# Unit 0 moves into the loop: decode attention and a Mish MLP, regrouped into even–odd passes

## The chip, the cores and the metric

The kernel runs on one core of a Trainium2 chip. Its time is device microseconds of one execution; the span is the part of it from the core's first to its last instruction. The engines named below are TensorE (PE), VectorE (DVE), ScalarE (ACT), GpSimd (POOL) and SyncE (SP). SP computes nothing here: it runs through its own list of instructions in order, and nearly every transfer from device memory is one of its instructions.

## The reference

One decode step for 8 sequences, everything in float32. `x` is 8 x 512; there are 32 query heads, 8 key/value heads, 8192 cached positions, and a head dimension of 128.

```python
xn = layernorm(x)
q  = xn @ wq                                    # 8 x 32 heads x 128
p  = softmax(q . k_cache * 128**-0.5)           # 4 query heads share one key head
a  = (p . v_cache) @ wo
h  = xn @ w1 + b1                               # 512 -> 1792
m  = (h * tanh(softplus(h))) @ w2               # Mish, 1792 -> 512
out = x + a + m
```

Each of the two caches is 268 MB and is read once; all weights together are some 24 MB.

## The kernel before, in words

**Units.** The caches are cut into 32 units, each of one sequence and two key/value heads. A unit has one key tile and one value tile of 128 x 16384 floats, 8.39 MB each, and each is one transfer. For a unit `u` the kernel does: `scores` (32 matmuls of 512 columns over the key tile, in two halves of 16, `part` 0 and 1), `softmax` (maximum, exponential, sums), `turn` (four matmuls and vector transposes that bring the weights into `pt8`), then `values` (32 matmuls over the value tile), then `merge` (division by the sum, into `oT`). `key_weights` lays the queries of the next unit out into the one buffer `wk`.

**Places.** One buffer `kv` of 160 KB per partition holds everything that is loaded. In units of one tile (`ROW`): the value place `V_AT` is 0 to 1; the keys of even units are at `K_AT[0]`, 1 to 2, those of odd units at `K_AT[1]`, 1.5 to 2.5. The two key places share half a tile, so a key tile may be loaded as soon as the first half of the scores of the unit before it has read the shared part; that is why `scores` is in two parts with the load between them.

**Order.** The schedule is written by hand. In a pass `t` of the loop SP meets, in order: the load of keys, the load of values, again keys, again values, with a wait ahead of each for the matmuls that still read the place. After unit 0, which stands ahead of the loop with `mish` (hidden layer of the MLP, 32 matmuls over `w1` and about 15 vector operations), a pass is an odd unit `2t+1` (`unit(t, 0, ..)`) and an even unit `2t+2` (`unit(t, 1, ..)`); in the last of the 16 passes the even unit is replaced by `last()`: values of unit 31, `wo` and `w2`. `values` of a unit run one unit later, behind the scores of the next: value tile `2t` is read in `unit(t, 0)`, and its successor `2t+1` is loaded right behind that.

**How waits are counted.** Each transfer of the loop adds 16 to one of eight counts when it has landed. The counts (`DMAHW0` to `DMAHW7` in the listings below, with `_I-..._own` for those of the loop and `_49` for those of the code ahead of it) are dealt out to the transfers of the program in turn, at build time. Every pass has to raise every count by the same amount. Where a block under an `If` has transfers and isn't taken, the other side of the branch makes up for them on SP: for each count it first waits until the transfers that the program has before on the same count have landed, then adds what the left-out block would have added.

**Ahead of the loop.** SP issues `x`, half of `wq`, key tile 0 (into the value place, L153), `w1` (into the first key place, L518), then key tile 1 into `K_AT[1]` and value tile 0 into `V_AT` (both at L534, in `load`).

Of the kernel before, what the change touches and what calls it, by code (L numbers as in the profile page):

```python
# [13 lines left out]
P = 128  # L14
# [41 lines left out]

V_AT = 0
K_AT = (ROW, ROW + ROW // 2)
W1_AT = ROW
W2_AT = 2 * ROW  # L60
PLACES = 2 * ROW + ROW // 2

# [14 lines left out]
def kernel(  # L77
# [72 lines left out]
    for lo in range(0, FG, FG // 2):  # L150
        hi = lo + FG // 2
        nc.scalar.dma_start(b1_sb[:, lo:hi], b1.rearrange("(g f) -> g f", g=G)[:, lo:hi])
    nc.sync.dma_start(kv[:, V_AT : V_AT + ROW], kT[:NB].rearrange("j p f -> (j p f)").rearrange("(p f) -> p f", p=P))  # L153
    w1_t = kv[:, W1_AT : W1_AT + 7168].rearrange("p (i f) -> p i f", i=W1R)


# [153 lines left out]
            nc.scalar.copy(qr[:, at].rearrange("p i c -> p (i c)"), X[:, half])  # L310

    wk = const.tile([P, DI, 2, NH * G, REP], F32, name="wk")
    lsel = const.tile([P, 2, H2], F32, name="lsel")
    qT = const.tile([P, H2 * B], F32, name="qT")

    def key_weights(b, parts=1):
        w = wk
        q = qr.rearrange("p i (d o h b) -> p i d o h b", d=2, o=1, b=B)[..., b]
        n = DI // parts
        for i in range(0, DI, n):  # L320
            nc.vector.tensor_mul(  # L321
                w[:, i : i + n],
                q[:, i : i + n].to_broadcast([P, n, 2, NH * G, REP]),
                mask.rearrange("p (o d k r) -> p o d k r", o=1, d=2, r=1).to_broadcast(
                    [P, n, 2, NH * G, REP]
                ),
            )


    def scores(j, k, first, part):  # L330

        w = wk
        lo = 0 if first else DI // 2
        kk = k.rearrange("p (i c f) -> p i c f", i=DI, c=HALF)
        for n in range(DI // 2):
            i = lo + n
            for c in range(HALF):
                nc.tensor.matmul(  # L338
                    S[64 * c : 64 * (c + 1), :],
                    w[:, i].rearrange("p d k h -> p (d k h)"),  # L340
                    kk[:, i, c, :],
                    start=(part == 0 and n == 0),
                    stop=(part == 1 and n == DI // 2 - 1),
                )

    E, RT = {}, {}

    def softmax(j):
        nm = work.tile([P, 1], F32, name="nm")
# [11 lines left out]
    def turn(j):  # L361
        e = E.pop(j)
        for g in range(4):
            nc.tensor.matmul(X[:, g], perm[:, g], e, start=True, stop=True)  # L364
        if j % 2 == 1:

            n = 2 * H2
            nc.tensor.matmul(  # L368
                M[:, 136 : 136 + n], ones, lsel.rearrange("p u h -> p (u h)"), start=True, stop=True
            )  # L370
            rt = work.tile([P, 2, H2], F32, name="rt")
            nc.vector.reciprocal(rt.rearrange("p u h -> p (u h)"), M[:, 136 : 136 + n])  # L372
            RT[0], RT[1] = rt[:, 0], rt[:, 1]
        for tl in range(TL):
            nc.vector.transpose(  # L375
                tr.rearrange("p (l t) c -> p t l c", t=TL)[:, tl],
                X.rearrange("p g (t q l) -> p t l g q", t=TL, q=PP)[:, tl],
            )
        t = tr.rearrange("p y (k z) -> p y k z", k=2)
        nc.vector.tensor_add(t[:, :, 0], t[:, :, 0], t[:, :, 1])  # L380
        for d in range(2):
            half = slice(64 * d, 64 * (d + 1))
            t = tr[half].rearrange("p y (g c h) -> p g y c h", g=4, c=HALF)
            nc.vector.tensor_add(  # L384
                pt8[half, :, :, d * REP : (d + 1) * REP].rearrange("p c y h -> p y c h"),
                t[:, 0],
                t[:, 1],
            )


    def values(vt):
        for n in range(NJ):
            l, c = divmod(n, HALF)
            q = n % G
            nc.tensor.matmul(  # L395
                O[Q * q : Q * (q + 1), :],
                pt8[:, c, TL * l : TL * (l + 1), :].rearrange("p t h -> p (t h)"),
                vt[:, 512 * n : 512 * (n + 1)],
                start=(n < G),
                stop=(n >= NJ - G),  # L400
            )
        os = work.tile([P, DH], F32, name="os")
        nc.vector.tensor_scalar(os, O[:, :DH], isel[:, 0:1], None, op0=ALU.mult)  # L403
        for i in range(1, TL):
            nc.vector.scalar_tensor_tensor(  # L405
                os, O[:, DH * i : DH * (i + 1)], isel[:, i : i + 1], os, op0=ALU.mult, op1=ALU.add
            )
        return os

    def merge(os, u, b):  # L410
        nc.tensor.matmul(M[:, 168 : 168 + H2], os, hsel, start=True, stop=True)  # L411
        nc.vector.tensor_mul(oT[:, :, b], M[:, 168 : 168 + H2], RT[u])

    def turn_o(m):

# [108 lines left out]
    def place(at):  # L524
        return kv[:, at : at + ROW]
# [7 lines left out]
    def load(name, at, m, b):  # L533
        nc.sync.dma_start(place(at), units[name][m, b])  # L534

    load("k", K_AT[1], 0, 1)
    scores(0, place(V_AT), True, 0)
    scores(0, place(V_AT), False, 1)
    softmax(0)
    load("v", V_AT, 0, 0)  # L540
    key_weights(1)
    mish(w1_t, b1_sb, kv[:, W1_AT : W1_AT + 6 * FG])
    turn(0)

    def last():

        w_o = [kv[:, 4096 * m : 4096 * (m + 1)] for m in range(NP)]
        for m in range(NP):
            rows = wo[4 * m : 4 * (m + 1)].rearrange("u p f -> (u p f)")
            rows = rows.rearrange("(p f) -> p f", p=P)  # L550
            nc.sync.dma_start(w_o[m], rows)
        w2_rows = w2.rearrange("j p f -> (j p) f").rearrange("(q i) f -> q (i f)", i=W2R)
        w2_t = []
        parts = ((0, G, 0, G), (G, 8, 0, G), (8, 11, 0, G), (11, 13, 0, G), (13, 14, 0, 2), (13, 14, 2, G))
        for lo, hi, g0, g1 in parts:
            a, z = (lo * D, hi * D) if g1 - g0 == G else (lo * D + g0 * P, lo * D + g1 * P)
            t = kv[:, W2_AT + a : W2_AT + z]
            nc.sync.dma_start(t, w2_rows[:, a:z])  # L558
            w2_t.append(t)

        os = values(place(K_AT[0]))
        for m in range(NP):
            if m == 1:
                merge(os, 1, B - 1)
                turn_o(NP - 1)
            outputs(m, w_o[m])
        down_long(w2_t[0])
        a_sb = work.tile([P, 512], F32, name="e", bufs=1)
        nc.scalar.copy(a_sb, H)
        for g in range(G):  # L570
            nc.tensor.matmul(
                O[Q * g : Q * g + B, :P],
                bsel[:, :B],
                a_sb[:, g * P : (g + 1) * P],
                start=True,
                stop=False,
            )
        for p, t in zip(parts[1:], w2_t[1:]):
            down(p[0], p[1], t, p[2], p[3])
        res = work.tile([P, DH], F32, name="os")  # L580
        nc.vector.tensor_add(res, O[:, :P], xres)  # L581
        nc.sync.dma_start(out, res)

    def unit(t, p, more):

        j = 1 + p
        scores(j, place(K_AT[(1 + p) % 2]), p == 0, 0)
        if p == 0:
            with tc.If(t < LOOPS - 1) as here:
                load("k", K_AT[0], (2 * t + 2) // B % NP, (2 * t + 2) % B)  # L590
            with here.Else():
                load("v", K_AT[0], NP - 1, B - 1)
        else:
            load("k", K_AT[1], (2 * t + 3) // B % NP, (2 * t + 3) % B)
        scores(j, place(K_AT[(1 + p) % 2]), p == 1, 1)
        softmax(j)
        os = values(place(V_AT))
        if p == 0:
            with tc.If(t % 4 == 0):
                turn_o((t // 4 + NP - 1) % NP)  # L600
            with tc.If(t < LOOPS - 1):
                load("v", V_AT, (2 * t + 1) // B % NP, (2 * t + 1) % B)
            with tc.If(more == 3):  # L603
                spread()
        else:
            load("v", V_AT, (2 * t + 2) // B % NP, (2 * t + 2) % B)
        key_weights((2 * t + 2 + p) % B)
        if p == 0:
            with tc.If(more == 2):  # L609
                project(tr.rearrange("p y c -> p (y c)")[:, :512])  # L610
        else:
            with tc.If(more == 1):
                load_q((t // 4 + 1) % NP)
        turn(j)
        merge(os, p, (2 * t + p) % B)

    with tc.For_i(0, LOOPS, hint_engines=(), iteration_sync="reg_based") as t:
        more = t % 4 + (t // 12) * 4
        unit(t, 0, more)
        with tc.If(t < LOOPS - 1) as here:  # L620
            unit(t, 1, more)
        with here.Else():
            last()


# [36 lines left out]
```

## Time and profile before

| | |
|---|---|
| median of three runs | 1315.33 us (1311.61 to 1317.71) |
| profiled execution, own time | 1311.87 us |
| its span | 1310.1 us |
| PE busy in the span | 1002.2 us, 77% |
| DVE busy | 359.2 us, 27% |
| bytes moved | 561.36 MB, mean 428 GB/s |

The profile is of one execution, with 1.8 us of its own time outside the span. An engine's busy time is a share of the whole span. The DMA figures are means over the core's 16 DMA engines, among which every transfer is split.

### The profile page before, as it was taken

The page shows a single profiled execution, that of the slowest core. Times are in us where ns is not written, and L with a number is a line of the kernel's source. Part 1 is how long each engine was busy: PE and PEld are TensorE (multiplying, and loading weights), DVE is VectorE, ACT ScalarE, POOL GpSimd, SP SyncE. Part 2 cuts the span into 40 slices and gives each one's busy share as a digit, 9 for nine tenths or more (in the row PEclk, how much of TensorE's full clock was granted, in tenths as well). Part 3 has the DMA queues.
Part 4 walks back from the last instruction along what each step waited for, and adds up shares of the span by engine and source line. Part 5 has one row for each costly group of instructions (what it writes and reads, how often), then busy time and mean ns, then how long its engine had stood idle before and what let it go on. Part 6 is the DMA issues. An engine that isn't in the chain of part 4 may idle for free. (4 is left out here: it accounts for less than half of the span.)

```text
span 1310.1 us, 13984 instructions
## 1 busy us (share of the span) xinstructions
PE 1002.2 (77%) x4948; PEld 348.9 (27%) x4948; DVE 359.2 (27%) x654; ACT 39.3 (3%) x89; POOL 2.3 (0%) x10
## 2 busy tenths in 40 slices
PE   5688687777877688687697877679688777868676
PEld 2233222222322222232232322223222222223222
DVE  3422232221323312233131323312233240323312
ACT  1000000000000000000000000000000000000000
POOL 0000000000000000000000000000000000000000
PEclk9898797988888898778797989788888897988788
DMA  9989999999999999999999999999999999999998
GB/s 405 443 377 425 437 430 433 432 431 434 431 431 434 426 440 424 442 424 446 422 440 426 436 430 436 434 430 436 430 436 428 434 430 440 430 434 434 430 423 349
DMA packets 11715, 561.36 MB, mean 428 GB/s; under 512 B 1312, under 2 KB 1704, under 8 KB 1968
## 3 DMA queue, kind: packets, MB, share of 16 engines
q1 hardware_dynamic: 11536, 560.03, 99.0%
q10 hardware_dynamic: 160, 1.06, 0.2%
q8 instruction: 15, 0.25, 0.1%
q14 instruction: 4, 0.03, 0.0%
HBM read 561.01 MB, written 0.07 MB: 428 GB/s over the span
## 5 line engine op out<-in xcount | busy, mean ns | idle before, releaser
L338 PE MATMUL s<-kv,wk 128*64 128x512 f32 x2048 | 530.7, 660 | 183.3 <-DMA kv<-in_kT 106.8
L338 PEld LDWEIGHTS s<-kv,wk 128*64 128x64 f32 x2048 | 176.8, 151 | 501.1 <-issue 415.7
L395 PE MATMUL o<-kv,pt 128*32 128x512 f32 x2048 | 254.1, 653 | 30.9 <-DMA kv<-in_v 26.1
L350 DVE TENSOR_REDUCE nm<-s 128x1 f32<-128x512 f32 x32 | 22.1, 692 | 548.0 <-issue 369.9
L364 PE MATMUL x<-e,perm 128*128 128x512 f32 x256 | 131.0, 659 | 17.9 <-PEq L609 15.9
L395 PEld LDWEIGHTS o<-kv,pt 128*32 128x32 f32 x2048 | 66.7, 119 | 194.6 <-issue 159.9
L375 DVE STREAM_TRANSPOSE tr<-x 128x512 f32<-128x512 f32 x128 | 80.3, 685 | 2.1
L364 PEld LDWEIGHTS x<-e,perm 128*128 128x128 f32 x256 | 51.0, 210 | 95.6 <-issue 88.8
L321 DVE TENSOR_TENSOR wk<-qr,mask 128x1024 f32<-128x1024 f32 (+1 forms) x34 | 64.8, 1905 | 33.2 <-DVEq L603 15.3
L403 DVE TENSOR_SCALAR os<-o,isel 128x128 f32<-128x128 f32 x32 | 11.2, 351 | 227.5 <-PE o L395 200.7
L358 ACT ACTIVATE e<-s,nmx 128x512 f32<-128x512 f32 x32 | 22.0, 687 | 1129.4 <-DVE nmx L355 1129.4
L384 DVE TENSOR_TENSOR pt<-tr 64x512 f32<-64x512 f32 x64 | 43.9, 686 | 2.2
L380 DVE TENSOR_TENSOR tr<-tr 128x1024 f32<-128x1024 f32 x32 | 39.2, 1225 | 1.1
L351 PE MATMUL m<-ident,nm 128*128 128x128 f32 x64 | 17.8, 364 | 26.3 <-DVE nm L350 26.3
L405 DVE SCALAR_TENSOR_TENSOR os<-o,isel,os 128x128 f32<-128x128 f32 x96 | 33.7, 351 | 3.4
L351 PEld LDWEIGHTS m<-ident,nm 128*128 128x128 f32 x64 | 10.9, 214 | 65.9 <-DVE nm L350 65.9
L303 PE MATMUL x<-tr,gwide 128*128 128x512 f32 x16 | 15.7, 1079 | 13.4 <-DVE tr L298 10.5
L275 PE MATMUL h<-ws,xn 128*8 128x512 f32 x64 | 10.9, 761 | 6.5 <-PEq L603 5.2
L359 DVE TENSOR_SCALAR lsel<-rsel,l 128x8 f32<-128x8 f32 x32 | 7.4, 231 | 29.8 <-ACT e L358 29.8
L411 PE MATMUL m<-hsel,os 128*128 128x8 f32 x64 | 10.9, 243 | 5.7 <-DVE rt L372 5.6
L353 DVE TENSOR_TENSOR far<-m,apart 128x128 f32<-128x128 f32 x32 | 9.3, 292 | 20.7 <-PE m L351 20.7
L411 PEld LDWEIGHTS m<-hsel,os 128*128 128x128 f32 x64 | 10.8, 189 | 15.3 <-issue 7.2
(103 smaller groups left out, 148.3 us busy)
## 6 DMA issues: line engine op xcount, KB each, us to landing
kv<-in_wo SPq DMA_DIRECT2D x4, 2048.0 KB, 20.2
ws<-in_wq SPq DMA_DIRECT2D x3, 2048.0 KB, 32.4
kv<-in_w SPq DMA_DIRECT2D x1, 3584.0 KB, 35.3
kv<-in_w SPq DMA_DIRECT2D x2, 1024.0 KB, 28.1
ws<-in_wq ACTq DMA_DIRECT2D x1, 1024.0 KB, 5.1
ws<-in_wq SPq DMA_DIRECT2D x1, 1024.0 KB, 7.2
kv<-in_w SPq DMA_DIRECT2D x1, 768.0 KB, 26.4
kv<-in_kT SPq DMA_DIRECT2D x32, 28.8
```

What stands on the lines that cost most here:

```text
L321: nc.vector.tensor_mul(w[:, i : i + n], q[:, i : i + n].to_broadcast([P, n, 2, NH * G, REP]), mask.rearrange("p (o d k r) -> p o d k r", o ...
L338: nc.tensor.matmul(S[64 * c : 64 * (c + 1), :], w[:, i].rearrange("p d k h -> p (d k h)"), kk[:, i, c, :], start=(part == 0 and n == 0), s ...
L350: nc.vector.tensor_reduce(nm, S, axis=AX.X, op=ALU.max, negate=True)
L351: nc.tensor.matmul(M[:, 0:P], nm.to_broadcast([P, P]), ident, start=True, stop=True)
L358: nc.scalar.activation(e, S, AF.Exp, bias=nmx, accum_out=l)
L364: nc.tensor.matmul(X[:, g], perm[:, g], e, start=True, stop=True)
L375: nc.vector.transpose(tr.rearrange("p (l t) c -> p t l c", t=TL)[:, tl], X.rearrange("p g (t q l) -> p t l g q", t=TL, q=PP)[:, tl],)
L380: nc.vector.tensor_add(t[:, :, 0], t[:, :, 0], t[:, :, 1])
L384: nc.vector.tensor_add(pt8[half, :, :, d * REP : (d + 1) * REP].rearrange("p c y h -> p y c h"), t[:, 0], t[:, 1],)
L395: nc.tensor.matmul(O[Q * q : Q * (q + 1), :], pt8[:, c, TL * l : TL * (l + 1), :].rearrange("p t h -> p (t h)"), vt[:, 512 * n : 512 * (n ...
L405: nc.vector.scalar_tensor_tensor(os, O[:, DH * i : DH * (i + 1)], isel[:, i : i + 1], os, op0=ALU.mult, op1=ALU.add)
L411: nc.tensor.matmul(M[:, 168 : 168 + H2], os, hsel, start=True, stop=True)
```

## The change

Unit 0 is no longer ahead of the loop. A pass is now the even unit `2t` (`unit(t, 0)`) and the odd unit `2t+1` (`unit(t, 1)`), so 16 passes hold all 32 units, and `last()` stands at the end under an `If` of its own that only pass 15 takes. What pass 0 must not do (values and merge of the unit before) or alone has to do (`mish`) is under an `If` too. The first key tile goes to the even keys' place, `w1` to the value place, and `mish` takes its work space in `ws`, where the query weights were. `os` and `rt` are fixed buffers now, since their readers stand in another pass.

```diff
-W1_AT = ROW
+W1_AT = 0
...
-    nc.sync.dma_start(kv[:, V_AT : V_AT + ROW], kT[:NB]...)
+    nc.sync.dma_start(kv[:, K_AT[0] : K_AT[0] + ROW], kT[:NB]...)
...
-    load("k", K_AT[1], 0, 1)
-    scores(0, place(V_AT), True, 0)
-    scores(0, place(V_AT), False, 1)
-    softmax(0)
-    load("v", V_AT, 0, 0)
-    key_weights(1)
-    mish(w1_t, b1_sb, kv[:, W1_AT : W1_AT + 6 * FG])
-    turn(0)
...
     def unit(t, p, more):
+        k = place(K_AT[p])
+        scores(k, p == 1, 0)
         if p == 0:
+            load("k", K_AT[1], (2 * t + 1) // B, (2 * t + 1) % B)
+        else:
             with tc.If(t < LOOPS - 1) as here:
                 load("k", K_AT[0], (2 * t + 2) // B % NP, (2 * t + 2) % B)
             with here.Else():
                 load("v", K_AT[0], NP - 1, B - 1)
-        else:
-            load("k", K_AT[1], (2 * t + 3) // B % NP, (2 * t + 3) % B)
+        scores(k, p == 0, 1)
+        softmax(p)
+        if p == 0:
+            with tc.If(t > 0):
+                values(place(V_AT))
+        else:
+            values(place(V_AT))
...
             with tc.If(t < LOOPS - 1):
-                load("v", V_AT, (2 * t + 1) // B % NP, (2 * t + 1) % B)
+                load("v", V_AT, (2 * t + 1) // B, (2 * t + 1) % B)
...
-            load("v", V_AT, (2 * t + 2) // B % NP, (2 * t + 2) % B)
-        key_weights((2 * t + 2 + p) % B)
+        key_weights((2 * t + 1 + p) % B)
+        if p == 0:
+            with tc.If(t == 0):
+                mish(w1_t, b1_sb, ws[:, : 6 * FG])
+            load("v", V_AT, (2 * t) // B, (2 * t) % B)
...
     with tc.For_i(0, LOOPS, hint_engines=(), iteration_sync="reg_based") as t:
         more = t % 4 + (t // 12) * 4
         unit(t, 0, more)
-        with tc.If(t < LOOPS - 1) as here:
-            unit(t, 1, more)
-        with here.Else():
+        unit(t, 1, more)
+        with tc.If(t == LOOPS - 1):
             last()
```

SP between the first key tile and the loop, before. An instruction stands with what it waits for; `PE_49` and the like are counts of an engine's finished instructions.

```order
L153 DMA kv<-in_kT 128x16384
L518 DMA kv<-in_w 128x7168
L534 DMA kv<-in_kT 128x16384 [waits DVE_49,DMAHW1_49,PE_49,Activation_49]
L534 DMA kv<-in_v 128x16384 [waits DMAHW5_49,DMAHW0_49,PE_49]
L617 COMPARE_AND_BRANCH [waits DMAHW0_I-317_own,DMAHW1_I-317_own,DMAHW2_I-317_own,DMAHW3_I-317_own,DMAHW4_I-317_own,DMAHW5_I-317_own,DMAHW6_I-317_own,DMAHW7_I-317_own]
L617 UNCONDITIONAL_BRANCH
```

The same stretch now, into the first rows of the loop (`load` is L535 here):

```order
L153 DMA kv<-in_kT 128x16384
L519 DMA kv<-in_w 128x7168
L617 COMPARE_AND_BRANCH [waits DMAHW0_I-209_own,DMAHW1_I-209_own,DMAHW2_I-209_own,DMAHW3_I-209_own,DMAHW4_I-209_own,DMAHW5_I-209_own,DMAHW6_I-209_own,DMAHW7_I-209_own]
L617 UNCONDITIONAL_BRANCH
L617 ISA
L535 ISA
L535 DMA kv<-in_kT 128x16384 [waits DMAHW1_I-209_own,DMAHW0_I-209_own,DMAHW2_I-209_own,PE_I-209_own,DMAHW3_I-209_own,DMAHW5_49,DMAHW4_I-209_own,DMAHW1_49,DMAHW5_I-209_own,DVE_49,DMAHW6_I-209_own,PE_49,Activation_49]
```

Key tile 1 has moved behind the loop's entry, where it is the load of odd keys of every pass; it now waits for 16 matmuls of the pass (`PE_I-209_own`: the first half of the scores of unit 2t).

SP at the end of a pass, before: the side of the branches at L612 and L620 that ends the even unit, ahead of the jump back. The four rows with waits raise the counts of what `last()` would have loaded. In this build the loads of the pass use `DMAHW0` (even keys), `DMAHW1` (odd values), `DMAHW2` (odd keys), `DMAHW3` (even values), `DMAHW4` (`wq`).

```order
L136 ISA [waits DMAHW4_I-317_own]
L136 DMA ws<-in_wq 128x4096 [waits DMAHW4_I-317_own,DMAHW2_49]
L612 UNCONDITIONAL_BRANCH
L612 REGISTER_ALU
L612 UNCONDITIONAL_BRANCH [waits DMAHW4_I-317_own]
L620 REGISTER_ALU
L620 REGISTER_ALU [waits DMAHW0_I-317_own]
L620 UNCONDITIONAL_BRANCH [waits DMAHW1_I-317_own,DMAHW5_I-317_own,DMAHW6_I-317_own,DMAHW7_I-317_own]
```

SP at the end of a pass now: the side of `If(t == LOOPS - 1)` that passes 0 to 14 go through, and the jump back. In this build the loads use `DMAHW0` (odd keys 2t+1), `DMAHW1` (even values 2t), `DMAHW2` (`wq`), `DMAHW3` (even keys 2t+2), `DMAHW4` (odd values 2t+1); `last()` has one or two loads on each of the eight.

```order
L621 UNCONDITIONAL_BRANCH
L621 REGISTER_ALU
L621 REGISTER_ALU [waits DMAHW0_I-209_own]
L621 REGISTER_ALU [waits DMAHW1_I-209_own]
L621 REGISTER_ALU [waits DMAHW2_I-209_own]
L621 REGISTER_ALU [waits DMAHW3_I-209_own]
L621 REGISTER_ALU [waits DMAHW4_I-209_own,DMAHW5_I-209_own,DMAHW6_I-209_own]
L621 UNCONDITIONAL_BRANCH [waits DMAHW7_I-209_own]
L617 ISA
L617 COMPARE_AND_BRANCH
```

Before, the counts waited for behind the pass's last load (even values, `DMAHW3`) were those of earlier loads; that load's own count was made up ahead of it, at L534. Now all eight stand in a row behind the last load (odd values, `DMAHW4`), and among them are that load's own count and that of the even keys ahead of it. The next transfer that SP issues is the odd keys of the next pass.

PE where a pass begins, now (`scores` is L343): the scores of the even unit.

```order
L617 COMPARE_AND_BRANCH [waits PE_I-209_own]
L617 UNCONDITIONAL_BRANCH
L343 MATMUL s<-kv,wk 64x512 [waits DVE_I-209_own,DMAHW0_I-209_own,Activation_I-209_own,DMAHW3_I-209_own,DMAHW5_49,DVE_49]
L343 MATMUL s<-kv,wk 64x512 x31
L356 REGISTER_ALU
L356 MATMUL m<-ident,nm 128x128 [waits DVE_I-209_own,DVE_49]
```

And before (`scores` is L338), the scores of the odd unit, with the jump over to the key load in their middle:

```order
L617 COMPARE_AND_BRANCH [waits PE_I-317_own]
L617 UNCONDITIONAL_BRANCH
L338 MATMUL s<-kv,wk 64x512 [waits DVE_I-317_own,DMAHW0_I-317_own,Activation_I-317_own,DMAHW2_I-317_own,DMAHW7_49,DVE_49]
L338 MATMUL s<-kv,wk 64x512 x15
L589 COMPARE_AND_BRANCH
L589 UNCONDITIONAL_BRANCH x2
L338 MATMUL s<-kv,wk 64x512 [waits DMAHW6_I-317_own]
L338 MATMUL s<-kv,wk 64x512 x3
```

The scores that open a pass are those of the even unit now, and of the transfers they wait for the even keys (`DMAHW3`) and the odd keys before them (`DMAHW0`).

More of the change, by code (lines that the diff above doesn't have):

```diff
@@ L152 @@
         nc.scalar.dma_start(b1_sb[:, lo:hi], b1.rearrange("(g f) -> g f", g=G)[:, lo:hi])
-    nc.sync.dma_start(kv[:, V_AT : V_AT + ROW], kT[:NB].rearrange("j p f -> (j p f)").rearrange("(p f) -> p f", p=P))
+    nc.sync.dma_start(
+        kv[:, K_AT[0] : K_AT[0] + ROW],
+        kT[:NB].rearrange("j p f -> (j p f)").rearrange("(p f) -> p f", p=P),
+    )
     w1_t = kv[:, W1_AT : W1_AT + 7168].rearrange("p (i f) -> p i f", i=W1R)
@@ L312 @@
     wk = const.tile([P, DI, 2, NH * G, REP], F32, name="wk")
+    os = const.tile([P, DH], F32, name="os")
+    rt = const.tile([P, 2, H2], F32, name="rt")
     lsel = const.tile([P, 2, H2], F32, name="lsel")
@@ L327, in key_weights, with scores @@
             )
-    def scores(j, k, first, part):
+    def scores(k, first, part):
         w = wk
@@ L344, in scores @@
                 )
-    E, RT = {}, {}
+    E = {}
     def softmax(j):
@@ L370, in turn @@
             )
-            rt = work.tile([P, 2, H2], F32, name="rt")
             nc.vector.reciprocal(rt.rearrange("p u h -> p (u h)"), M[:, 136 : 136 + n])
-            RT[0], RT[1] = rt[:, 0], rt[:, 1]
         for tl in range(TL):
@@ L401, in values @@
             )
-        os = work.tile([P, DH], F32, name="os")
         nc.vector.tensor_scalar(os, O[:, :DH], isel[:, 0:1], None, op0=ALU.mult)
@@ L407, in values, with merge @@
             )
-        return os
-    def merge(os, u, b):
+    def merge(u, b):
         nc.tensor.matmul(M[:, 168 : 168 + H2], os, hsel, start=True, stop=True)
-        nc.vector.tensor_mul(oT[:, :, b], M[:, 168 : 168 + H2], RT[u])
+        nc.vector.tensor_mul(oT[:, :, b], M[:, 168 : 168 + H2], rt[:, u])
     def turn_o(m):
@@ L559, in last @@
             w2_t.append(t)
-        os = values(place(K_AT[0]))
+        values(place(K_AT[0]))
         for m in range(NP):
             if m == 1:
-                merge(os, 1, B - 1)
+                merge(1, B - 1)
                 turn_o(NP - 1)
@@ L579, in last @@
             down(p[0], p[1], t, p[2], p[3])
-        res = work.tile([P, DH], F32, name="os")
+        res = os
         nc.vector.tensor_add(res, O[:, :P], xres)
@@ L584, in unit @@
     def unit(t, p, more):
-        j = 1 + p
-        scores(j, place(K_AT[(1 + p) % 2]), p == 0, 0)
+        k = place(K_AT[p])
+        scores(k, p == 1, 0)
         if p == 0:
+            load("k", K_AT[1], (2 * t + 1) // B, (2 * t + 1) % B)
+        else:
             with tc.If(t < LOOPS - 1) as here:
@@ L592, in unit @@
                 load("v", K_AT[0], NP - 1, B - 1)
-        else:
-            load("k", K_AT[1], (2 * t + 3) // B % NP, (2 * t + 3) % B)
[L595 to L598, printed above, removed]
+        scores(k, p == 0, 1)
[3 more added lines that the diff above has]
+                values(place(V_AT))
+        else:
+            values(place(V_AT))
             with tc.If(t % 4 == 0):
@@ L601, in unit @@
             with tc.If(t < LOOPS - 1):
-                load("v", V_AT, (2 * t + 1) // B % NP, (2 * t + 1) % B)
+                load("v", V_AT, (2 * t + 1) // B, (2 * t + 1) % B)
             with tc.If(more == 3):
                 spread()
-        else:
-            load("v", V_AT, (2 * t + 2) // B % NP, (2 * t + 2) % B)
-        key_weights((2 * t + 2 + p) % B)
-        if p == 0:
+        key_weights((2 * t + 1 + p) % B)
[3 more added lines that the diff above has]
+            load("v", V_AT, (2 * t) // B, (2 * t) % B)
+            with tc.If(more == 2):
+                load_q((t // 4 + 1) % NP)
+        else:
             with tc.If(more == 2):
                 project(tr.rearrange("p y c -> p (y c)")[:, :512])
-        else:
[L612 to L615, printed above, removed]
+        turn(p)
+        if p == 0:
+            with tc.If(t > 0):
+                merge(1, (2 * t + B - 1) % B)
+        else:
+            merge(0, (2 * t) % B)
     with tc.For_i(0, LOOPS, hint_engines=(), iteration_sync="reg_based") as t:
```

## Prediction

> **What bounds the kernel now.** I read the page first, its sections 1 to 3, then the rates of chosen stretches, the list of SP's transfers in order of time, and the landing of single transfers.
>
> ```profile
> span 1310.1 us, 13984 instructions
> ...
> PE 1002.2 (77%) x4948; PEld 348.9 (27%) x4948; DVE 359.2 (27%) x654; ACT 39.3 (3%) x89; POOL 2.3 (0%) x10
> ...
> q1 hardware_dynamic: 11536, 560.03, 99.0%
> ...
> L338 PE MATMUL s<-kv,wk 128*64 128x512 f32 x2048 | 530.7, 660 | 183.3 <-DMA kv<-in_kT 106.8
> ```
>
> Transfers take 99% of the span; the largest group of PE work is 530.7 us, 16.6 us for each of 32 units, and it waits for keys. So DMA bounds it, and what counts is any time in which the transfer queue runs dry. The rates by stretch (last two columns: share of the 16 DMA engines, GB/s) tell whether it does:
>
> ```profile
> 98.00:1277.00 1179.00, 912.45 (x4361) 315.25 (x4362) 313.45 (x546) 30.36 (x72) 0.00 (x0) 0.86 1.00 433
> 73.00:74.00 1.00, 1.00 (x8) 0.43 (x6) 0.00 (x0) 0.00 (x0) 0.00 (x0) 1.00 0.16 66
> 74.00:75.00 1.00, 1.00 (x8) 0.33 (x6) 0.00 (x0) 0.00 (x0) 0.00 (x0) 1.00 0.01 0
> ...
> 75.50:77.90 2.40, 2.40 (x14) 0.92 (x12) 0.00 (x0) 0.00 (x0) 0.00 (x0) 1.00 0.00 0
> 74.25:77.95 3.70, 3.70 (x20) 1.38 (x18) 0.00 (x0) 0.00 (x0) 0.00 (x0) 1.00 0.11 35
> ```
>
> From 98 to 1277 us the rate is 433 GB/s at a full share, so a tile of 8.39 MB takes 8.39 / 0.433 = 19.4 us and there is nothing to win in the loop. The one hole is near 75 us; the next packets start between 77.90 and 77.95. The transfers around it, and the scores:
>
> ```profile
> 2.08 0.75 SPq L518 DMA_DIRECT2D kv<-in_w  x1
> 27.86 15.36 PE L338 MATMUL s<-kv,wk 128*64 128x512 f32 x64 [3.07 <-DMA kv<-in_kT]
> 43.25 0.33 SPq L534 DMA_DIRECT2D kv<-in_v  x1
> ...
> 45.28 6.20 PE L444 MATMUL h<-kv,oX 128*8 128x448 f32 x64
> ...
> 67.46 16.03 PE L338 MATMUL s<-kv,wk 128*64 128x512 f32 x64 [12.35 <-DVEq L617]
> 76.95 0.36 SPq L534 DMA_DIRECT2D kv<-in_kT  x1
> 92.09 0.35 SPq L534 DMA_DIRECT2D kv<-in_v  x1
> 110.09 0.34 SPq L534 DMA_DIRECT2D kv<-in_kT  x1
> ```
>
> Key tile 2 was issued at 76.95, since the scores of unit 1 began only at 67.46: PE stood 12.35 us at the loop's entry until DVE had come through `mish` (DVEq L617). Landings (us from issue) of value tile 0 (issued 43.2), key tile 2 (76.9), value tile 1 (92.1), and of `w1` in the page's list:
>
> ```profile
> L534 SPq DMA_DIRECT2D kv<-in_v x1: 328/328/328, 43.2 to 43.2; - x1
> DMA to landing us min/median/max: 32.6/32.6/32.6
> ...
> L534 SPq DMA_DIRECT2D kv<-in_kT x1: 358/358/358, 76.9 to 76.9; - x1
> DMA to landing us min/median/max: 23.1/23.1/23.1
> ...
> L534 SPq DMA_DIRECT2D kv<-in_v x1: 347/347/347, 92.1 to 92.1; - x1
> DMA to landing us min/median/max: 27.3/27.3/27.3
> ...
> kv<-in_w SPq DMA_DIRECT2D x1, 3584.0 KB, 35.3
> ```
>
> Value tile 0 landed at 43.25 + 32.6 = 75.9, key tile 2 at 76.95 + 23.1 = 100.05. That is 24.2 us for 19.4 us of data: the hole cost 4.8 us. Against that, value tile 1 landed at 92.09 + 27.3 = 119.4, and the odd keys behind it had been issued at 110.09, 9.3 us ahead: that lead is why the loop shows no hole.
>
> **The change, part by part.**
>
> *Start.* The 12.35 us wait goes: the scores of unit 1 no longer stand behind the loop's entry, so DVE's 15 operations of `mish` lie beside the landing of key tile 1 and value tile 0. Late next is key tile 1. It was free to go early (its place was empty); now it waits for the first half of the scores of unit 0. These begin at 27.86 and half of 15.36 us is 7.7, so it is issued near 36 us with the entry's branches, and first packets follow the issue by 77.9 - 76.95 = 0.95 us. Ahead of it `w1` is done at 2.08 + 35.3 = 37.4 on the last DMA engine. The new hole lies between 0 (all engines as late as the last) and 36 + 23.1 - 37.4 - 19.4 = 2.3 us; I take 1.8, near the upper row, since it was measured on a dry queue. Key tile 2 then no longer waits: -4.8 + 1.8 = **-3.0 us**, bounds -4.8 and 0. Value tile 0 now waits until `mish` has read `w1` on PE, which before was at 45.28 + 6.20 = 51.5 us; key tile 1 is in flight until at least 36 + 0.95 + 19.4 = 56, so no hole follows.
>
> *End of every pass.* SP now has, behind the load of the odd values, the made-up counts of `last()`. Among them is `DMAHW4`, raised by that very load, and `DMAHW3`, raised by the even keys before it. SP goes in order, so in passes 0 to 14 it stands until the odd values have landed, and only then comes to the load of the odd keys. That load is the next in the queue and nothing else is queued: the 9.3 us of lead turn into a dry queue, 15 times. Before, the same kind of wait was at L620, on loads long consumed:
>
> ```profile
> L620 SPq EVENT_SEMAPHORE  x75: 17/17/17, 129.5 to 1231.1; - x75
> ```
>
> 75 waits in 15 passes, none longer than 17 ns. The Trainium skill, "DMA: Bandwidth & Descriptors", section "Anatomy of one DMA — SWDGE (gpsimd) path", says that DMA engines never wait on semaphores, the issuing sequencer does, before dispatch; its section "Rules for kernel authors" asks to issue early and wait late. Both speak against this change, and the trace's 110.09 (issued ahead) against 119.4 (landed) agrees with them.
>
> The price of one dry queue is SP's way from the landing to the issue, and the transfer's start. SP's way, from the pass end of the same trace (x, duration, first and last start):
>
> ```profile
> L620 SPq EVENT_SEMAPHORE  x5: 17/17/17, 129.5 to 129.8; - x5
> L617 SPq MOVE  x1: 38/38/38, 130.6 to 130.6; - x1
> L534 SPq FUSED_REGOPS  x2: 96/138/180, 130.8 to 131.0; - x2
> L534 SPq EVENT_SEMAPHORE  x1: 28/28/28, 131.1 to 131.1; - x1
> ```
>
> From the last made-up count (129.8) through the jump back to the load's first wait (131.1) it takes 1.3 us, 0.1 of it a branch that is now gone. Three more counts and six waits at some 0.07 us (five in 0.3) add 0.55: **1.75 us**. The start has two bounds. Above: 23.1 us from issue to landing on a dry queue, 19.4 of it data, so 3.7. But in that stretch code was being fetched for the loop's first pass, which delays single DMA engines. Below: 0.95 us to the first packets, plus a slow first packet. The rates show it: 16 packets start near 77.9, the next not before 81.
>
> ```profile
> 80.00:81.00 1.00, 1.00 (x8) 0.34 (x6) 0.00 (x0) 0.00 (x0) 0.00 (x0) 1.00 0.00 0
> 81.00:82.00 1.00, 1.00 (x6) 0.31 (x4) 0.00 (x0) 0.00 (x0) 0.00 (x0) 1.00 2.42 1049
> q8 instruction: 15, 0.25, 0.1%
> ```
>
> That is at least 3.1 us where later packets take 2.42 (the share column: each of 16 engines 2.42 us for one packet); so 0.95 + 0.8 = 1.75. The sixteen engines also have to meet at each pass's end, and the spread between them is lost. One dry queue costs 1.75 + 1.75 = 3.5 to 1.75 + 3.7 = 5.5. I take **4.3**: nearer the lower row, with 0.8 for the spread, because the 15 code fetches of the page can touch only some passes. 15 x 4.3 = **+64.5 us** (52.5 to 82.5).
>
> *The rest costs nothing.* More branches per pass and the drains of PE, DVE and ACT in skipped blocks lie in engines that wait for data anyway (PE is 77% busy), and each pass gives them 4.3 us more. If that cover went, a branch would cost 0.1 to 0.3 us by SP's rows above; with some ten a pass that is at most 48 us, all bare. `load_q`, `project` and `spread` stay at the same units. Value tile 2t waits for the skipped `mish`, behind a key tile of 19.4 us. The tail keeps its order of loads, with the wait for unit 31's values ahead of the same piece of `w2`.
>
> Sum: 1311.87 - 3.0 + 64.5 = 1373.4 us for the profiled execution. The median of the runs was 3.5 us above that execution, so I name 1376 for the median.
>
> **The rivals.**
>
> *The new waits are free (not slower).* If the counts waited for belonged to loads that had landed, as at L620, only the start would change: 1311.87 - 3.0 = 1309, and no more than 4.8 can be won. It decides by whether odd keys are issued before the odd values have landed. For it speaks that the same construct cost 17 ns a piece 75 times; against it, that the load whose count is waited for is issued directly ahead, some 27 us from landing.
>
> *A lone transfer's cost is all that a dry queue costs.* The output, 64 KB on an empty queue, took 1.6 us from issue to landing:
>
> ```profile
> out<-os SPq DMA_DIRECT2D x1, 64.0 KB, 1.6
> ```
>
> If SP's way hid behind late DMA engines and nothing but this remained, 15 x 1.6 - 3.0 = +21, 1333 us. Against it: SP can't start before the last engine's landing. The Trainium skill (same page, "Anatomy of one DMA — SWDGE (gpsimd) path") fits 2.0 us fixed plus the bytes, for the other descriptor path; as an estimate from it, 15 x 2.0 - 3.0 gives 1339. The 3.7 us of key tile 2 is more than either.
>
> *PE starts late as well.* If the scores that open a pass also hung on the last made-up counts, their first half (16.6 / 2 = 8.3 us) would stand between landing and issue instead of 1.75: 6.5 us more in each pass, 1373 + 98 = 1471. Against it: they wait for `DMAHW0` and `DMAHW3`, which SP raises before it comes to `DMAHW4`.
>
> **How the numbers follow.** A measurement of this kernel tells about 0.5%, 6.6 us, from no change. Forecast 0.84; free waits 0.07, of which nearly all lies within 0.5%; lone transfer 0.05; late PE 0.04. Faster by over 0.5% would need more than the 4.8 us that the start can give: 0.02, out of the free waits. Within: 0.05. Slower: 0.93. The range takes the forecast's bounds: 1311.87 - 4.8 + 52.5 = 1360, less 2 for the reading of SP's way; and 1311.87 + 0 + 82.5 + 3.5 = 1398.
>
> **What would show it.** Rates: holes once per pass, 15 of them, about 78 + 4.3 us apart, the one near 75 gone, one of under 2 us near 36. SP's waits at the `If` of `last()`: some 15 long ones for transfers of values. Odd keys issued about 1.75 us behind a landing, and landing 21 to 23 us later; even keys and all values still some 28. PE's wait at the loop's entry under 3 us. If odd keys are still issued ahead of the odd values' landing, the prediction is wrong at its main step; if the holes are there but of another size, at the price.

## The result

The changed kernel takes 1371.68 us (median of 6 runs, 1371.13 to 1371.95). The kernel before takes 1315.05 us beside it (6 runs, 1311.61 to 1317.71). The ratio is 1.0431, with an interval of 1.0415 to 1.0447: slower by 4.3%. The profiled execution took 1371.78 us, 59.9 more than that of before; its span is 1369.6. The kernel before took some 1313 us in 40 more runs beside the experiments below; a 41st, of 1954.5 us, is left out of their ratios.

From the page of the changed kernel, the same parts that were read before:

```profile
span 1369.6 us, 14588 instructions
...
PE 978.0 (71%) x4948; PEld 354.8 (26%) x4948; DVE 360.3 (26%) x654; ACT 39.3 (3%) x89; POOL 2.3 (0%) x10
...
q1 hardware_dynamic: 11536, 560.03, 95.4%
...
L343 PE MATMUL s<-kv,wk 128*64 128x512 f32 x2048 | 510.6, 662 | 221.6 <-DMA kv<-in_kT 162.6
...
kv<-in_w SPq DMA_DIRECT2D x1, 3584.0 KB, 35.0
```

The same bytes move in the same number of packets, and PE's work is no longer than before; only the queue's share fell, from 99.0 to 95.4%. The idle time of the scores for want of keys went from 106.8 to 162.6 us. So most of the time went into stretches in which nothing moved. The rates by stretch (last two columns: DMA share, GB/s; a packet counts where it starts) show them:

```profile
120.00:1240.00 1120.00, 799.56 (x3964) 291.19 (x3968) 284.42 (x497) 28.80 (x68) 0.00 (x0) 0.87 0.96 412
...
36.70:38.50 1.80, 1.80 (x11) 0.62 (x8) 0.00 (x0) 0.00 (x0) 0.00 (x0) 1.00 0.00 0
38.50:38.60 0.10, 0.10 (x2) 0.00 (x0) 0.00 (x0) 0.00 (x0) 0.00 (x0) 1.00 6.05 1966
...
118.90:121.80 2.90, 1.94 (x16) 0.71 (x18) 1.27 (x3) 0.32 (x1) 0.00 (x0) 1.00 0.00 0
121.80:121.90 0.10, 0.10 (x4) 0.00 (x0) 0.00 (x0) 0.10 (x1) 0.00 (x0) 1.00 9.64 3277
...
1274.40:1277.25 2.85, 2.20 (x12) 0.69 (x16) 0.23 (x1) 0.76 (x2) 0.00 (x0) 0.54 0.00 0
```

One hole stands near 37 us, and the 15 others, of which the first and the last are shown, each stand at the end of a pass and last 2.8 to 3.0 us, some 43 us together. (The tail has one of 2.2 us ahead of the output, as it had before.) The row behind a hole shows where more is lost: five packets of 65.5 KB start in that tenth of a microsecond (3277 GB/s x 0.1 us), and they take 0.1 x 16 x 9.64 / 5 = 3.1 us each, where the prediction's row has 2.42. Who stands while the queue is dry, in the list of SP's waits (total us, times, longest):

```profile
SPq L621 <- SPq L621: 446.4, 30, 19.5
```

L621 is the `If` of `last()`. 30 waits are two in each of 15 passes: for the even keys and for the odd values. Before, no row of this list named the corresponding line. SP's transfers in order of time, and from issue to landing those of value tile 1 (issued 88.86) and of the odd keys behind it (120.88):

```profile
37.55 0.35 SPq L535 DMA_DIRECT2D kv<-in_kT  x1
...
70.59 0.34 SPq L535 DMA_DIRECT2D kv<-in_kT  x1
88.86 0.34 SPq L535 DMA_DIRECT2D kv<-in_v  x1
120.88 0.34 SPq L535 DMA_DIRECT2D kv<-in_kT  x1
```

```profile
L535 SPq DMA_DIRECT2D kv<-in_kT x1: 348/348/348, 37.5 to 37.5; - x1
DMA to landing us min/median/max: 23.0/23.0/23.0
...
L535 SPq DMA_DIRECT2D kv<-in_v x1: 337/337/337, 88.9 to 88.9; - x1
DMA to landing us min/median/max: 30.5/30.5/30.5
...
L535 SPq DMA_DIRECT2D kv<-in_kT x1: 343/343/343, 120.9 to 120.9; - x1
DMA to landing us min/median/max: 21.9/21.9/21.9
```

Value tile 1 landed at 88.86 + 30.5 = 119.36. The odd keys were issued 1.52 us behind that, and landed at 142.78: 23.42 us after the landing ahead, for 19.4 us of data. One dry queue costs 4.0 us, and 15 of them 60, which is the whole difference between the two profiled executions (59.9). The start adds nothing: value tile 1 landed at 119.4 in the kernel before as well.

PE at the start, and where the 12.35 us wait at the loop's entry had been:

```profile
28.01 15.99 PE L343 MATMUL s<-kv,wk 128*64 128x512 f32 x64 [3.03 <-DMA kv<-in_kT]
...
60.68 1.98 PE L343 MATMUL s<-kv,wk 128*64 128x512 f32 x4 [3.81 <-DMA kv<-in_kT]
```

The scores of unit 1 begin at 60.68 instead of 67.46, and wait for their keys and no longer for DVE. Key tile 2 is issued at 70.59 instead of 76.95, well ahead of need.

### The profile page after: what moved, and what is told of

The parts are those of the page before. It is cut to its first block, busy times and chain, and to the rows that moved or that the text cites. A ratio compares the mean times of both kernels' runs of the same rounds, so it can differ in the third digit from the quotient of the medians.

```text
span 1369.6 us, 14588 instructions
## 1 busy us (share of the span) xinstructions
PE 978.0 (71%) x4948; PEld 354.8 (26%) x4948; DVE 360.3 (26%) x654; ACT 39.3 (3%) x89; POOL 2.3 (0%) x10
## 2 busy tenths in 40 slices
DMA packets 11707, 561.21 MB, mean 410 GB/s; under 512 B 1313, under 2 KB 1705, under 8 KB 1969
## 3 DMA queue, kind: packets, MB, share of 16 engines
q1 hardware_dynamic: 11536, 560.03, 95.4%
## 5 line engine op out<-in xcount | busy, mean ns | idle before, releaser
L343 PE MATMUL s<-kv,wk 128*64 128x512 f32 x2048 | 510.6, 662 | 221.6 <-DMA kv<-in_kT 162.6
L343 PEld LDWEIGHTS s<-kv,wk 128*64 128x64 f32 x2048 | 175.0, 153 | 533.1 <-issue 528.4
L398 PE MATMUL o<-kv,pt 128*32 128x512 f32 x2048 | 258.1, 661 | 57.4 <-DMA kv<-in_v 26.3
L369 PE MATMUL x<-e,perm 128*128 128x512 f32 x256 | 123.9, 629 | 34.5 <-PEq L608 13.9
L398 PEld LDWEIGHTS o<-kv,pt 128*32 128x32 f32 x2048 | 80.8, 120 | 211.5 <-issue 206.6
L378 DVE STREAM_TRANSPOSE tr<-x 128x512 f32<-128x512 f32 x128 | 80.3, 684 | 19.9 <-PE x L369 19.4
```

The source lines that it names most:

```text
L343: nc.tensor.matmul(S[64 * c : 64 * (c + 1), :], w[:, i].rearrange("p d k h -> p (d k h)"), kk[:, i, c, :], start=(part == 0 and n == 0), s ...
L378: nc.vector.transpose(tr.rearrange("p (l t) c -> p t l c", t=TL)[:, tl], X.rearrange("p g (t q l) -> p t l g q", t=TL, q=PP)[:, tl],)
L398: nc.tensor.matmul(O[Q * q : Q * (q + 1), :], pt8[:, c, TL * l : TL * (l + 1), :].rearrange("p t h -> p (t h)"), vt[:, 512 * n : 512 * (n ...
```

## The experiments

The theory on trial: SP stands at the pass's end for a transfer that was issued directly ahead, and so the next load is issued into an empty queue. The rivals: the new place of the `If` or its many branches cost the time; the start costs it; PE's or DVE's share of a pass costs it. Each kernel below differs in one respect from the changed kernel, from the kernel before, or from an experiment that stands ahead of it. The first five are about the ends of the passes, the last two about the start.

**last7: `last()` without a transfer on the count of the odd values.** The program and the place of the `If` stay as in the changed kernel. `last()` loads the same bytes in 7 transfers instead of 11, and so raises seven counts; `DMAHW4`, that of the odd values, is not among them and isn't made up.

```diff
-        for m in range(NP):
-            rows = wo[4 * m : 4 * (m + 1)]...
-            nc.sync.dma_start(w_o[m], rows)
+        for m in range(0, NP, 2):
+            rows = wo[4 * m : 4 * (m + 2)]...
+            nc.sync.dma_start(kv[:, 4096 * m : 4096 * (m + 2)]..., rows)
-        parts = ((0, G, 0, G), (G, 8, 0, G), (8, 11, 0, G), (11, 13, 0, G), (13, 14, 0, 2), (13, 14, 2, G))
+        parts = ((0, G, 0, G), (G, 8, 0, G), (8, 12, 0, G), (12, 14, 0, G))
```

> The changed kernel with 7 transfers in last() instead of 11 (wo in two, w2 in four, the output), so that they use the counts DMAHW5, 6, 7, 0, 1, 2 and 3, and no longer DMAHW4, the count of the odd values. Nothing else is changed: all branches, skipped blocks and drains stay. Theory (SP stands at the pass end until the odd values have landed, because their count has to be made up): the 15 dry queues of some 4 us vanish, about 1371.7 - 60 + 1 for the coarser tail = 1313 us. Rival (the branches, skipped blocks and drains of the new pass cost the time): 1371 us as before.

1310.84 us (1309.90 to 1314.37), ratio 0.9977 [0.9967, 0.9987]: the whole loss is gone, and a little more. Rates by stretch, and the landing of value tile 1 and of the odd keys behind it:

```profile
120.00:1240.00 1120.00, 843.39 (x4172) 308.46 (x4170) 304.15 (x528) 29.63 (x70) 0.00 (x0) 0.88 1.00 433
```

```profile
L535 SPq DMA_DIRECT2D kv<-in_v x1: 338/338/338, 89.8 to 89.8; - x1
DMA to landing us min/median/max: 29.9/29.9/29.9
...
L535 SPq DMA_DIRECT2D kv<-in_kT x1: 343/343/343, 116.5 to 116.5; - x1
```

The odd keys are issued at 116.5, and the values ahead of them land at 89.8 + 29.9 = 119.7: 3.2 us of lead, no hole, 433 GB/s again. SP still stands 15 times at L621, for the even keys; that wait is free, since the odd values are queued behind those.

```profile
SPq L621 <- SPq L621: 155.8, 15, 15.2
```

**last8: one transfer more, on that count.** As last7, but the last 1024 columns of `w2` come in two pieces. The output, the eighth transfer, then takes `DMAHW4`.

```diff
-        parts = ((0, G, 0, G), (G, 8, 0, G), (8, 12, 0, G), (12, 14, 0, G))
+        parts = ((0, G, 0, G), (G, 8, 0, G), (8, 12, 0, G), (12, 13, 0, G), (13, 14, 0, G))
```

> As last7, but with one transfer more in last(): the last 1024 columns of w2 come in two pieces, so that the eighth transfer, the output, takes DMAHW4. Theory: one 64 KB transfer in a block that only the last pass takes brings back all 15 dry queues, 1372 us, some 58 us more than last7. Rival (it is not the counts): within 2 us of last7, whichever way that comes out.

1372.92 us (1371.65 to 1373.63), ratio 1.0447 [1.0420, 1.0473]. The stall is back in full:

```profile
SPq L621 <- SPq L621: 438.0, 30, 19.5
```

```profile
L535 SPq DMA_DIRECT2D kv<-in_v x1: 333/333/333, 90.4 to 90.4; - x1
DMA to landing us min/median/max: 29.7/29.7/29.7
...
L535 SPq DMA_DIRECT2D kv<-in_kT x1: 348/348/348, 121.6 to 121.6; - x1
DMA to landing us min/median/max: 21.8/21.8/21.8
```

Landing at 90.37 + 29.7 = 120.07, next issue 121.58, 1.51 us later. The two kernels differ by one transfer, which only the last pass runs and which moves the output onto `DMAHW4`; in the other 15 passes that is nothing but a wait and an addition. This is the pair that settles the cause: 62 us hang on one made-up count, with loop, branches, order of work and bytes the same.

**two_sides: no made-up counts behind the loads.** The odd unit is written twice, once for passes 0 to 14 and once, with `last()`, for pass 15. With `end=True` the unit loads the last values in place of keys and leaves out what pass 15 doesn't take; that part of the edit isn't printed.

```diff
...
-        unit(t, 1, more)
-        with tc.If(t == LOOPS - 1):
+        with tc.If(t < LOOPS - 1) as here:
+            unit(t, 1, more)
+        with here.Else():
+            unit(t, 1, more, end=True)
             last()
```

> The changed kernel with the odd unit written out twice, under If(t < LOOPS - 1) and, with last() behind it, under its Else; so the counts of even keys and odd values are made up ahead of these loads, where the transfers before them landed long ago. All 11 transfers stay. But the fifth piece of w2 lies in the odd keys' place and counts on DMAHW4 like the odd values, so the load of the odd keys has a wait of its own for that count from the pass before. Theory (any wait ahead of that load for the odd values dries the queue; only SP's way of 1.55 us from landing to issue gets shorter, to about 0.2): 15 x 1.35 = 20 us less, about 1351 us. Rival (the made-up counts at the pass end are the only cause): 1312 us. Rival (the branches): 1371 us.

1352.32 us (1351.97 to 1352.84), ratio 1.0294 [1.0268, 1.0320]. Two thirds of the loss stay, as expected, and for another reason. A piece of `w2` that `last()` loads on `DMAHW4` lies in the place of the odd keys, so the load of the odd keys itself waits for that count in every pass. The wait stands now at the load, behind the jump back (30 waits for values at L535, where the changed kernel has 15):

```profile
SPq L535 <- DMA kv<-in_v: 272.9, 30, 11.7
```

```profile
169.72 0.34 SPq L535 DMA_DIRECT2D kv<-in_v  x1
199.60 0.34 SPq L535 DMA_DIRECT2D kv<-in_kT  x1
```

```profile
L535 SPq DMA_DIRECT2D kv<-in_v x1: 338/338/338, 169.7 to 169.7; - x1
DMA to landing us min/median/max: 29.7/29.7/29.7
```

Landing at 169.72 + 29.7 = 199.42, next issue at 199.60: SP's way is 0.2 us instead of 1.5. The saving over the changed kernel, (1371.7 - 1352.3) / 15 = 1.3 us a pass, is that way. So a dry queue has two parts: the way, which depends on where the wait stands in the code, and some 2.7 us that stay with the way at nearly nothing: (1352.3 - 1311.0) / 15, against sides_wo2 below.

**sides_wo2: neither wait.** two_sides with `wo` in two transfers. The pieces of `w2` move to other counts, and only the output is left on `DMAHW4`.

```diff
-        for m in range(NP):
+        for m in range(0, NP, 2):
...
```

> two_sides with wo in two transfers instead of four: the six pieces of w2 then count on DMAHW6, 7, 0, 1, 2, 3 and only the output on DMAHW4, and the odd keys have no wait for the odd values' count any more, made up or own. Theory: no dry queue at the pass ends, 1352 - 15 x 2.6 = 1313 less at most 1, so 1311 to 1314. Rival (a further cause is left in the new passes): above 1318.

1311.01 us (1309.91 to 1314.32), ratio 0.9982 [0.9973, 0.9991], 433 GB/s from 120 to 1240 us:

```profile
120.00:1240.00 1120.00, 850.31 (x4174) 310.81 (x4172) 304.14 (x528) 29.62 (x70) 0.00 (x0) 0.88 1.00 433
```

With both waits for the odd values away, nothing of the loss is left.

**own_if: the `If` alone, in the kernel before.** Unit 0 stays ahead of the loop; only `last()` gets an `If` of its own in place of the `Else`.

```diff
-        with tc.If(t < LOOPS - 1) as here:
+        with tc.If(t < LOOPS - 1):
             unit(t, 1, more)
-        with here.Else():
+        with tc.If(t == LOOPS - 1):
             last()
```

> The kernel before, with unit 0 ahead of the loop and passes of an odd and an even unit, and one change: last() stands under an If of its own behind the even unit instead of under the Else of it. Theory: the even values' count (DMAHW3) now has to be made up behind their load, and the next even keys wait for SP: 15 dry queues of some 4 us, 1315 + 60 = 1375 us. Rival (the regrouping with unit 0 in the loop is what costs): 1315 us.

1379.97 us (1379.78 to 1380.99), ratio 1.0503 [1.0477, 1.0529]: the stall needs nothing of the regrouping. It is 5 us dearer than expected:

```profile
L534 SPq DMA_DIRECT2D kv<-in_v x1: 341/341/341, 131.1 to 131.1; - x1
DMA to landing us min/median/max: 29.2/29.2/29.2
...
L534 SPq DMA_DIRECT2D kv<-in_kT x1: 333/333/333, 162.2 to 162.2; - x1
```

Landing at 131.13 + 29.2 = 160.33, issue at 162.24: SP's way is 1.9 us here. The 0.4 us more than in the changed kernel, 15 times, are 6 us. The start differs too in this execution:

```profile
79.09 0.35 SPq L534 DMA_DIRECT2D kv<-in_kT  x1
```

Key tile 2 was issued 2.1 us later than in the kernel before (76.95), and landed 2.2 us later. Against the 1313 us of the kernel before beside it, the excess over 60 is 7 us; 6 and 2.2 fit that in size. Neither was tried by itself.

**start_only: the start alone, in the kernel before.** Key tile 0 in the even keys' place, `w1` in the value place, key tile 1 behind the first half of the scores of unit 0, `mish` in `ws`; unit 0 stays ahead of the loop, and the loop is that of before.

```diff
-W1_AT = ROW
+W1_AT = 0
...
-    load("k", K_AT[1], 0, 1)
-    scores(0, place(V_AT), True, 0)
-    scores(0, place(V_AT), False, 1)
+    scores(0, place(K_AT[0]), False, 0)
+    load("k", K_AT[1], 0, 1)
+    scores(0, place(K_AT[0]), True, 1)
     softmax(0)
-    load("v", V_AT, 0, 0)
     key_weights(1)
-    mish(w1_t, b1_sb, kv[:, W1_AT : W1_AT + 6 * FG])
+    mish(w1_t, b1_sb, ws[:, : 6 * FG])
+    load("v", V_AT, 0, 0)
```

> The kernel before with the start of the changed one alone: key tile 0 in the even keys' place, w1 in the value place, key tile 1 issued behind the first half of unit 0's scores, value tile 0 behind mish; unit 0 stays ahead of the loop and PE still waits for DVE at the loop's entry. In the changed kernel the hole of some 5 us ahead of key tile 2 gave way to one of some 4 us ahead of key tile 1. Theory (the two holes don't add: later key and value tiles cover PE's wait at the entry): value tile 1 lands within 1.5 us of its 119.4 before, the time within 2 us of before. Rival (they add): 4 us slower, 1318 to 1319, value tile 1 landing near 123.

1313.30 us (1311.43 to 1317.76), ratio 1.0005 [0.9994, 1.0017]: no change. The new hole near 37 us takes what the old one near 75 gives back. In the profiled execution, which at 1314.26 us is 2.4 longer than that of the kernel before, value tile 1 landed at 121.1 us (issued at 93.64, 27.5 us to landing): 1.7 us later than before, a little more than the 1.5 that were expected, and short of the rival's 123. Key tile 2 isn't early here, since `mish` still stands ahead of the scores of unit 1:

```profile
37.46 0.33 SPq L534 DMA_DIRECT2D kv<-in_kT  x1
...
78.35 0.35 SPq L534 DMA_DIRECT2D kv<-in_kT  x1
```

**early_half: the start's hole filled.** sides_wo2, with key tile 1 in two halves. The upper half of its place is never shared with key tile 0, so that half is loaded ahead of the loop, behind `w1`; pass 0 loads only the lower half.

```diff
+    nc.sync.dma_start(
+        kv[:, K_AT[1] + ROW // 2 : K_AT[1] + ROW], units["k"][0, 1][:, ROW // 2 :]
+    )
...
-            load("k", K_AT[1], (2 * t + 1) // B, (2 * t + 1) % B)
+            with tc.If(t > 0) as later:
+                load("k", K_AT[1], (2 * t + 1) // B, (2 * t + 1) % B)
+            with later.Else():
+                nc.sync.dma_start(
+                    kv[:, K_AT[1] : K_AT[1] + ROW // 2], units["k"][0, 1][:, : ROW // 2]
+                )
```

> sides_wo2, with key tile 1 in two halves: the upper half of its place, which key tile 0 doesn't share, is loaded ahead of the loop, the lower half in pass 0 where the whole tile was. Theory: 4.2 MB more are queued behind w1, so the hole of some 4 us ahead of key tile 1 closes and nothing else moves: 4 us below sides_wo2, about 1308, the fastest of all. Rival (the hole moves on to value tile 0 or key tile 2, as it moved before): within 1 us of sides_wo2.

1310.63 us (1307.37 to 1312.00), ratio 0.9974 [0.9964, 0.9984], 0.4 us below sides_wo2 where 4 were expected, and with intervals that overlap. In the trace the hole is gone, and no other has opened ahead of the tail: the rival's figure came out, but not its mechanism. SP's transfers in sides_wo2, and the landing of value tile 0:

```profile
37.88 0.35 SPq L535 DMA_DIRECT2D kv<-in_kT  x1
53.84 0.35 SPq L535 DMA_DIRECT2D kv<-in_v  x1
...
1306.21 0.35 SPq L574 DMA_DIRECT2D out<-os  x1
```

```profile
DMA to landing us min/median/max: 26.7/26.7/26.7
```

And in early_half:

```profile
24.82 0.33 SPq L537 DMA_DIRECT2D kv<-in_kT  x1
37.01 0.33 SPq L588 DMA_DIRECT2D kv<-in_kT  x1
53.69 0.36 SPq L535 DMA_DIRECT2D kv<-in_v  x1
...
1304.31 0.35 SPq L578 DMA_DIRECT2D out<-os  x1
```

```profile
DMA to landing us min/median/max: 24.7/24.7/24.7
```

Value tile 0 lands at 78.4 instead of 80.5: 2.1 us of the expected 4, by the last of the 16 DMA engines. By the median of the engines it ended 3.5 us earlier, but the last engine trails the median by 3.1 us in early_half and by 1.9 in sides_wo2, and a landing counts with the last. The output then goes out 1.9 us earlier in these two executions. Why the medians of 12 and 10 runs are only 0.4 us apart stays open, as does what the spread among the engines comes from.

last7, sides_wo2 and early_half are each 0.2 to 0.3% faster than before. That is at the edge of what can be told, and the trace of sides_wo2 (1311.86 us) doesn't differ from that of before (1311.87). What these 2 to 3 us of the medians are was not traced.

## Why the prediction was right, step by step

*The main step held.* SP stands at the made-up counts for the odd values; 15 dry queues, one in each of passes 0 to 14, at the ends of passes, and nowhere else in the loop. Odd keys land 21.9 us from their issue (21 to 23 named). last7 and last8 show that the made-up count in flight decides; two_sides shows that the load's own wait for that count does the same. One sign did not come: values were to land some 28 us from their issue, and their median is 33.3, value tile 2 taking 34.0. Value tile 2 was issued only 7.2 us behind the odd keys, and so waits for most of them; the sum doesn't hang on it.

*The price of a dry queue: 4.0 us, 4.3 taken.* SP's way was 1.52 instead of 1.75. The rest, from issue to landing beyond the data, is 21.9 - 19.4 = 2.5 us, against 2.55 as the sum of the three smaller pieces (0.95 to the first packets, 0.8 for a slow first packet, 0.8 for the spread). The first packets started between 121.80 and 121.90, 0.9 to 1.0 us behind the issue. The Trainium skill, "DMA: Bandwidth & Descriptors", section "Latency and other measured facts", puts the first byte on this descriptor path at about 0.6 us; from the start of the issue the trace shows more, and counted from the end of the 0.34 us issue it agrees. The first packet took 3.1 us on the five engines that start it by 121.90, so 0.7 more than later ones, near the 0.8 taken. The third piece has no row behind it in the prediction, and the trace shows another in its place: the 16 first packets don't start together, seven start between 121.90 and 122.30 and the last four by 122.80, 1.9 us behind the issue. The spread at the landing ahead isn't part of this stretch, since SP's wait ends with the last engine. That 2.55 met 2.5 is luck in this third. 15 x (4.0 - 4.3) is -4.5 us against the named sum.

*The start was mis-sized: -3.0 taken, -0.74 by the same working with the measured rows.* The formula was issue + landing time - end of `w1` - 19.4. With what happened it is 37.55 + 23.0 - (2.09 + 35.0) - 19.4 = 4.06 for the new hole, where 1.8 was taken and 2.3 was the upper bound; and -4.8 + 4.06 = -0.74. Read directly it is nothing: value tile 1 lands at 119.4 in both kernels. The step that failed is the time of the issue: half of the scores' duration, 7.7 us, was added to their start. The load waits for the 16th matmul, and that isn't the middle of the bar. Of its 64 records, two for each matmul, only 28 had started after 8.0 us, and the 32nd ended 9.1 us behind the start, at a granted clock of 1.00 throughout; why the first matmuls run slower is open. SP's own way behind the wait is under 0.4 us. The wait can be seen in the trace (min/median/max ns of SP's wait instructions at the load):

```profile
L535 SPq EVENT_SEMAPHORE  x5: 28/28/32861, 4.3 to 37.4; - x5
```

32.86 us from 4.3 end at 37.2, 9.2 us behind the start of the scores at 28.01. The rows to see it stood in the prediction: scores at 67.46, key tile 2 issued at 76.95, 9.49 us for the same half. 27.86 + 9.49 = 37.35 would have been right within 0.2 us. The two errors have opposite signs: +2.26 and -4.5. The sum with the measured terms is 1311.87 - 0.74 + 60 = 1371.1, and the profiled execution took 1371.78. For the median 3.5 us more were named, since the runs of the kernel before lay that far above its profiled execution. Those did not come: the runs of the changed kernel lie within 0.8 us, and their median is 0.1 below the profiled one, so 1376 was too high by 4.3.

*PE's wait.* Under 3 us was named at the loop's entry; it is 3.03 there, and 3.81 at the scores of unit 1. Both wait for keys, and the second holds the hole of the start.

*The rest at nothing.* Branches and skipped blocks cost nothing that could be found: last7 has them all and is not slower than before.

*The rivals.* Free waits are out: they do occur, for the even keys in last7, 155.8 us in all at no cost, but the odd values' count is in flight with nothing queued behind. A lone transfer's cost alone is out by two_sides: even with SP's way at 0.2 us a dry queue costs some 2.7 us, not 1.6. Late PE is out too: 8.3 us of scores would stand between landing and issue, and 1.52 do.

*One piece of evidence that could not carry what it was quoted for.* The 75 waits of 17 ns at L620 were given as proof that those waits were free. The same view of the changed kernel, where SP stood 446.4 us at that place, reads no differently:

```profile
L621 SPq EVENT_SEMAPHORE  x120: 17/17/17, 90.3 to 1275.1; - x120
```

Such a stand isn't in the duration of these wait instructions; it is in the list of waits. The Trainium skill, "Perfetto Trace Analysis", section "Per-instruction lifecycle: what the profiler-reported window actually captures", says that a sequencer's instruction is reported from the time its semaphores are satisfied. The trace agrees at L621 and not at L535, where one wait of 32861 ns is in the duration; so that view can show a stand and can't show that there was none. That the old waits were free holds all the same, since that list of before has no row for L620. A second thing the prediction left out is the load's own wait for `DMAHW3` and `DMAHW4`: by two_sides it alone would have dried the queue at 1352 us, had the made-up counts been cheap.

## What to carry to other kernels

Where transfers are the bound, look at each wait on the issuing engine and ask what is still queued behind the transfer that it waits for: here a wait for the last transfer in the queue cost the engine's way to the next issue plus that transfer's start (1.5 + 2.5 us), once per pass; a wait for the one before it was free in last7. When a block under an `If` changes its number of transfers or its place, see which counts it shares with loads in flight: in last8 one transfer more, which only the last pass runs, cost 62 us in the other fifteen. To foretell when a transfer waiting for half of a group is issued, take the measured distance from an earlier occurrence, not half of the bar: the first half of the matmuls took 9.1 of 16.0 us.

## What was not expected of the hardware

A dry queue brings the 16 DMA engines together again: value tile 1 of the changed kernel ended on the last of them 1.8 us behind their median, and the odd keys that were issued into the empty queue 0.4 us behind it. In the passes after that it stayed between 0.2 and 0.7 us. In three kernels without dry queues the spread hardly moved from key tile 3 on, 1.0 us in sides_wo2, 2.1 in early_half and 2.4 to 2.5 in last7. That isn't a rule: in the kernel before it went between 0.4 and 1.8 us along the loop, and what moved it wasn't traced. So a gain at the start that is read from the median engine can be smaller on the last one, as in early_half.
